# Attention over a small state and a squared-ReLU feed-forward layer on one core: sums of w_out blocks on VectorE, some squares on ScalarE, a new written order from the third batch on

## The chip, the cores and the metric

The kernel runs on one core of a Trainium2 chip. The metric is the device time of one execution in microseconds (us). TensorE (PE) multiplies, VectorE (DVE), ScalarE (ACT) and GpSimd (POOL) do the elementwise work, SyncE (SP) issues nearly all DMAs. A difference of about 0.3% is what a measurement of this kernel can tell from none.

## The reference, cut to what matters

```python
# attention: B, H, S, Ns, D = 8, 8, 512, 32, 64
scores = scale * x @ state.T                 # a = softmax(scores); xread = a @ state
scores2 = scale * state @ x.T                # a2 = softmax(scores2); sread = a2 @ x
x = concat([xread, sread], axis=2)           # 8 x 8 x 544 x 64 -> 4352 x 512
# feed-forward: d_model 512, d_ff 2048
h = maximum(x @ w_in, 0.0)
out = (h * h) @ w_out
```

All data are float32. The weights come to the chip as 64-bit floats and are turned into 32-bit ones there.

## The kernel before, in words

The rows of one batch (512 tokens, xread) are a block, numbered 0 to 7; the 256 sread rows of all batches are block 8. TensorE multiplies in a reduced 32-bit format, so each factor is split: hi is the rounded value (a copy on ScalarE), lo is the remainder (one subtraction on VectorE or GpSimd), and a product is hi*hi + hi*lo + lo*hi, three matmuls.

For a block, `hidden(blk, fc)` makes 128 of the 2048 hidden columns (fc counts to 16): six matmuls of 128x512 into `ph`, ReLU on ScalarE into `r`, the square, and the split into `g_hi` and `g_lo`. `accumulate(blk, fc)` multiplies them by 128 rows of w_out (`wo`) into four accumulators. This is done for blocks 0 to 4 and 8; block 8 is worked on between 4 and 5.

Blocks 5 to 7 use seven products in place of eight, as in Strassen's scheme. Once blocks 4 and 8 no longer need two neighbouring `wo` blocks, `sums.p` (`add_weights(p)`, p from 0 to 7) turns them into sums and differences `v`, `sv`, `one`, and splits these in place into `wo`, `both` and `first` (or `two_first`). That is nine operations on VectorE or GpSimd for each p and four casts on ScalarE. `hidden_fast` leaves the squares in a tile `g`; `fast.blk.p.h` (`accumulate_fast`, h is 0 or 1) makes the matching sums of `g` in a tile `s` (f_sum 256, d_sum 256 and e_sum 128 columns) and the remainders `a_g_lo` (p_lo and f_lo, 256 columns each) and `b_g_lo` (b_lo, 384 columns), and issues 21 matmuls of 128x256 into `m`. A step 5.3 in the text is block 5, p = 3, and 5.3.0 its half h = 0.

What runs in which order: `PLAN` is a list of step names; each time a name stands in it, that step's function runs to its next `yield`. So PLAN sets the order in which instructions are written, and a scheduler keeps most of it. Each engine works through its own instructions in order. `SECOND` is a table of keys: an operation whose key stands in it goes to the second engine of its `pick(key, first, second)`. Before the change `add_weights` picks GpSimd first and no key of it stands in the table, and the sums in `accumulate_fast` pick VectorE first, again without a key. The profile names line 408, a wrapper, for every instruction, so tiles tell what an instruction is.

Of the kernel before, what the change touches and what calls it, by code (L numbers as in the profile page):

```python
# [122 lines left out]
        accumulate.1.15 accumulate.1.15 load.3.1 hidden.2.0 hidden.2.0 hidden.2.3 hidden.2.0 hidden.2.0
        accumulate.1.15 accumulate.1.15 load.3.1 load.3.1 accumulate.1.15 accumulate.1.15 hidden.2.3 hidden.2.3
        hidden.2.3 split_wf.4 accumulate.1.15 accumulate.2.0 hidden.2.3 hidden.2.3 prep.3.0 split_wf.4 later_w2.4
        later_w2.4 load.3.1 later_w2.4 later_w2.4 accumulate.2.1 exp_s.2.1 transposes.2 hidden.2.2 transposes.2
        load_wf.1.6 later_w2.4 later_w2.4 later_w2.4 hidden.2.2 hidden.2.2 hidden.2.2 load_w2.2.3 load.4.1
# [5 lines left out]
        hidden.2.5 transposes.2 split_wf.7 split_wf.6 later_w2.6 split_wf.7 later_w2.6 split_wf.7 later_w2.6
        later_w2.6 later_w2.6 later_w2.6 later_w2.6 split_wf.7 load_wf.2.1 later_w2.6 later_w2.6 accumulate.2.5
        load_w2.2.4 load_w2.2.4 later_w2.7 later_w2.7 later_w2.7 later_w2.7 later_w2.7 later_w2.7 later_w2.7
        accumulate.2.6 hidden.2.9 hidden.2.9 load.4.1 load.4.1 hidden.2.9 hidden.2.9 hidden.2.9 hidden.2.9
        hidden.2.7 sread.1 hidden.2.7 hidden.2.7 load_w2.2.5 hidden.2.7 read.2 load_w2.2.6 hidden.2.7 hidden.2.7
        sread.2 load.4.1 sread.2 sread.2 hidden.2.8 hidden.2.8 hidden.2.8 hidden.2.8 later_w2.7 hidden.2.8
        hidden.2.8 accumulate.2.7 w2.1+scores.3 last_w2.1 transposed_scores.3.0 exp_s.3.0 accumulate.2.8 later_w2.7
        last_w2.1 sread.2 start.5 start.5 load_wf.2.0 start.5 start.5 load_w2.2.5 last_w2.1 last_w2.1 load_w2.2.6  # L140
        last_w2.1 load_w2.2.5 hidden.2.11 hidden.2.11 hidden.2.11 load.5.1 softmax.3.0 hidden.2.11
        transposed_scores.3.1 softmax.3.1 load_w2.2.6 exp_s.3.1 prep.4.1 hidden.2.10 hidden.2.10 hidden.2.11
        hidden.2.11 softmax.3.0 softmax.3.0 softmax.3.0 load.5.1 hidden.2.10 load_w2.2.7 load_w2.3.1 hidden.2.10
        load.5.1 load.5.1 softmax.3.1 load_n.3.0 softmax.3.1 hidden.2.10 hidden.2.10 accumulate.2.9 exp_s.3.1
        softmax.3.1 exp_s.3.0 exp_s.3.0 exp_s.3.1 prep.4.0 hidden.2.13 hidden.2.12 hidden.2.12 hidden.2.13
        hidden.2.13 hidden.2.13 transposes.3 transposes.3 hidden.2.13 hidden.2.13 load_w2.2.7 load_w2.3.0
        load_w2.3.1 accumulate.2.10 load_w2.2.7 accumulate.2.11 hidden.2.14 last_w2.1 hidden.2.12 hidden.2.12
# [5 lines left out]
        prep.5.0 transposes.3 start.6 start.6 load_wf.2.5 softmax.3.1 hidden.3.0 start.6 hidden.2.15 hidden.2.15
        hidden.2.15 softmax.4.0 softmax.4.0 softmax.4.0 accumulate.2.14 exp_s.4.0 hidden.3.2 hidden.3.0 hidden.3.0
        hidden.3.0 hidden.3.0 hidden.3.0 accumulate.2.15 accumulate.2.15 accumulate.2.15 accumulate.2.15
        accumulate.2.15 start.6 exp_s.4.1 load_w2.3.2 exp_s.4.1 exp_s.4.0 exp_s.4.0 transposes.4 transposes.4
        softmax.4.0 load_w2.3.2 softmax.4.0 hidden.3.1 accumulate.2.15 hidden.3.1 hidden.3.1 read.3 sread.3 sread.3
        sread.3 accumulate.2.15 accumulate.2.15 hidden.3.1 hidden.3.1 hidden.3.1 prep.5.1 softmax.4.0 softmax.4.0
        hidden.3.2 hidden.3.2 hidden.3.2 hidden.3.2 hidden.3.2 load.6.1 load_n.4.0 softmax.4.1 transposes.4
        load_w2.3.4 softmax.4.1 load_w2.3.3 transposes.4 load.6.1 accumulate.3.0 accumulate.3.1 softmax.4.1  # L160
        softmax.4.1 hidden.3.3 hidden.3.3 hidden.3.3 load.6.1 hidden.3.3 hidden.3.3 hidden.3.3 hidden.3.4
        load_w2.3.5 hidden.3.4 hidden.3.4 load.6.1 accumulate.3.2 load_w2.3.3 hidden.3.4 hidden.3.4 hidden.3.4
        transposes.4 softmax.4.1 softmax.4.1 w2.2+scores.5 last_w2.2 last_w2.2 transposed_scores.5.0 accumulate.3.3
        load_n.4.1 load_w2.3.4 softmax.4.1 hidden.3.5 last_w2.2 last_w2.2 last_w2.2 last_w2.2 exp_s.5.0 softmax.5.0
        transposed_scores.5.1 exp_s.5.0 exp_s.5.1 softmax.5.0 load_w2.3.5 softmax.5.1 load_w2.3.5 hidden.3.7
        prep.6.0 hidden.3.5 hidden.3.5 exp_s.5.1 exp_s.5.1 hidden.3.5 hidden.3.5 hidden.3.5 hidden.3.7
        accumulate.3.4 load_w2.3.4 softmax.5.0 start.7 hidden.3.7 hidden.3.7 hidden.3.7 hidden.3.7 w2.5+read.4
# [5 lines left out]
        accumulate.3.7 softmax.5.1 last_w2.3 last_w2.3 last_w2.3 transposes.5 hidden.3.9 hidden.3.9
        transposed_scores.6.0 transposed_scores.6.1 exp_s.6.1 exp_s.6.1 softmax.5.1 softmax.5.1 softmax.6.1
        load_w2.3.7 hidden.3.9 hidden.3.9 hidden.3.11 load_w2.3.7 hidden.3.11 hidden.3.9 hidden.3.9 hidden.3.11
        load_w2.4.0 load_w2.4.1 accumulate.3.8 exp_s.6.0 softmax.6.0 softmax.6.0 hidden.3.11 hidden.3.11
        hidden.3.11 exp_s.6.0 hidden.3.10 hidden.3.10 load_w2.3.7 hidden.3.10 exp_s.6.0 transposes.5 load.7.1
# [1389 lines left out]
```

## Time and profile before

| | |
|---|---|
| three runs | 681.49, 683.40, 683.48 us; median 683.4 |
| profiled execution | 680.74 us, span from first to last instruction 679.0 us |
| TensorE busy | 647.4 us (95%) |
| VectorE busy | 502.0 us (74%) |
| ScalarE busy | 379.8 us (56%) |
| GpSimd busy | 217.2 us (32%) |
| DMA | 113.07 MB, mean 167 GB/s |

Busy time is the union of an engine's instructions. A share over the whole span is a mean of stages with different limits; the rows below are taken by stage. Consecutive instructions of VectorE overlap a little, so the distance between two starts is shorter than the duration of one.

### The profile page before, as it was taken

How to read it: one execution, taken by the hardware profiler on the slowest of the kernel's cores; microseconds unless marked ns; L12 is line 12 of the kernel's file. 1: busy time of each engine (PE TensorE's matmuls, PEld its weight loads, DVE VectorE, ACT ScalarE, POOL GpSimd, SP SyncE). 2: the span in 40 equal slices, each digit the busy share in tenths (PEclk: the TensorE clock that was granted, in tenths of full speed). 3: DMA queues.
4: the chain of work that ended last, by engine and by line, in shares of the span. 5: the costliest groups of instructions: out<-in, count | busy, mean ns of one | idle time of the engine just before them, and what ended most of it. 6: DMA issues, size and time to landing. Idle time of an engine off the chain costs nothing. (4 is left out here: it accounts for less than half of the span.)

```text
span 679.0 us, 12256 instructions
## 1 busy us (share of the span) xinstructions
PE 647.4 (95%) x4453; PEld 534.0 (79%) x4453; DVE 502.0 (74%) x951; ACT 379.8 (56%) x790; POOL 217.2 (32%) x173
## 2 busy tenths in 40 slices
...
GB/s 300 305 252 270 274 223 303 275 259 259 173 290 244 196 281 221 218 263 128 318 232 125 48 70 149 65 40 52 41 22 46 94 67 121 100 57 154 63 1 63
DMA packets 153132, 113.07 MB, mean 167 GB/s; under 512 B 93168, under 2 KB 126448, under 8 KB 153072
## 3 DMA queue, kind: packets, MB, share of 16 engines
...
q10 hardware_dynamic: 288, 0.26, 0.1%
q14 instruction: 25, 0.20, 0.1%
...
## 5 line engine op out<-in xcount | busy, mean ns | idle before, releaser
L408 PE MATMUL acc<-wo,g_hi 128*128 128x512 f32 x704 | 204.0, 393 | 0.0
L408 PE MATMUL ph<-k_hi,w 128*128 128x512 f32 x512 | 179.9, 401 | 2.2 <-DVE w L408 1.6
L408 PEld LDWEIGHTS acc<-wo,g_hi 128*128 128x128 f32 x704 | 130.6, 188 | 32.8 <-ACT w2h L408 2.5
L408 PE MATMUL acc<-wo,g_lo 128*128 128x512 f32 x352 | 122.2, 392 | 0.1
L408 PEld LDWEIGHTS ph<-k_hi,w 128*128 128x128 f32 x512 | 97.9, 192 | 25.9 <-DVE w L408 2.3
L408 PE MATMUL ph<-k_lo,w 128*128 128x512 f32 x256 | 102.0, 398 | 0.0
L408 ACT ACTIVATE r<-ph 128x512 f32<-128x512 f32 (+1 forms) x91 | 52.8, 580 | 78.7 <-PE ph L408 69.8
L408 DVE TENSOR_TENSOR g_lo<-ph,g_hi 128x512 fp32r<-128x512 f32 (+1 forms) x95 | 60.4, 639 | 37.7 <-ACT g_hi L408 33.6
L408 ACT ACTIVATE ph<-ph 128x512 f32<-128x512 f32 (+1 forms) x106 | 58.3, 550 | 37.4 <-PE ph L408 28.2
L408 PEld LDWEIGHTS acc<-wo,g_lo 128*128 128x128 f32 x352 | 65.7, 188 | 15.5 <-DVE g_lo L408 0.9
L408 POOL TENSOR_TENSOR w<-w_f,w 128x512 fp32r<-128x512 f32 x23 | 30.4, 1326 | 118.9 <-ACT w L408 118.9
L408 PEld LDWEIGHTS ph<-k_lo,w 128*128 128x128 f32 x256 | 49.2, 192 | 8.3
L408 DVE SCALAR_TENSOR_TENSOR ph<-ph,r 128x512 f32<-128x512 f32 (+1 forms) x43 | 27.9, 649 | 34.1 <-ACT r L408 33.8
L408 DVE TENSOR_TENSOR g<-r 128x512 f32<-128x512 f32 x48 | 41.0, 865 | 11.4 <-ACT r L408 11.2
L408 POOL TENSOR_TENSOR o<-s,s 128x256 f32<-128x256 f32 x2 | 1.4, 728 | 131.6 <-ACT s L408 131.6
L408 POOL TENSOR_TENSOR sp<-sp,m 128x512 f32<-128x512 f32 x20 | 21.5, 1074 | 37.4 <-DVE m L408 34.1
L408 POOL TENSOR_TENSOR wf<-wf,wf_hi 128x512 fp32r<-128x512 f32 x11 | 14.6, 1332 | 56.4 <-ACT wf_hi L408 46.1
L408 ACT CAST g_hi<-ph 128x512 fp32r<-128x512 f32 (+1 forms) x53 | 29.2, 551 | 4.1 <-PE acc L408 2.8
L408 ACT ACTIVATE g_hi<-r 128x512 fp32r<-128x512 f32 (+1 forms) x43 | 25.7, 597 | 6.7 <-PE acc L408 4.3
L408 POOL TENSOR_TENSOR s<-sf,s 128x512 fp32r<-128x512 f32 x11 | 14.1, 1292 | 43.2 <-ACT s L408 42.7
L408 ACT CAST w<-w_f 128x512 fp32r<-128x512 f32 x40 | 24.2, 615 | 3.1 <-DMA w_f<-w_d 2.1
L408 POOL TENSOR_SCALAR dec<-wo_raw 128x512 f32<-128x512 f32 x10 | 21.0, 2103 | 13.0 <-DMA wo_raw<-in_moe_w_out_dram 12.8
...
## 6 DMA issues: line engine op xcount, KB each, us to landing
...
```

The lines of the kernel that those rows point to most:

```text
L408: op = call(*args, **kw)
```

## The change

In `add_weights` the two engines of each `pick` change places: VectorE is the first, GpSimd the second. New keys `v`, `sv` and `sv_lo` send 13 of the 72 operations to GpSimd. New keys `f_sum`, `d_sum`, `e_sum`, `p_lo`, `f_lo` and `b_lo` send 93 of the 288 operations of `accumulate_fast` to GpSimd. New keys `g_sq` send 24 of the 48 squares of blocks 5 to 7 to ScalarE. Some other splits change engines, and PLAN is another list from line 119 of the file on (late in block 1). The rest of the code does the same as before.

```diff
 SECOND = """
+    b_lo: 5.6.1 6.0.0 6.0.1 6.2.1 6.3.0 6.5.0 6.6.0 6.7.0 7.2.1 7.4.0
+    d_sum: 5.3.0 5.4.0 6.0.0 6.1.0 6.1.1 6.2.1 6.4.0 6.5.1 6.6.0 7.0.1 7.1.1 7.3.0 7.4.0 7.4.1 7.5.0 7.5.1 7.6.0
...
+    g_sq: 5.0 5.1 5.2 5.3 5.4 5.5 5.6 5.7 5.8 5.9 5.10 5.11 5.12 5.13 5.14 5.15 6.0 6.1 6.2 6.3 6.6 6.7 6.8 6.11
...
+    sv: 0.2 1.1 1.2
+    sv_lo: 0.0 0.1 0.2 0.3 1.3 2.1 2.3 5.1 7.0
+    v: 0.0
...
-            pick(f"v.{p}.{i}", nc.gpsimd, nc.vector).tensor_add(v[:, i], w[:, 0].bitcast(F32), w[:, 1].bitcast(F32))
-            yield
-        pick(f"sv.{p}.0", nc.gpsimd, nc.vector).tensor_sub(s[:, 0], v[:, 0], v[:, 1])
...
+            pick(f"v.{p}.{i}", nc.vector, nc.gpsimd).tensor_add(v[:, i], w[:, 0].bitcast(F32), w[:, 1].bitcast(F32))
+            yield
+        pick(f"sv.{p}.0", nc.vector, nc.gpsimd).tensor_sub(s[:, 0], v[:, 0], v[:, 1])
...
-            pick(f"sv_lo.{p}.{i}", nc.gpsimd, nc.vector).tensor_sub(w[:, 1], a, w[:, 0].bitcast(F32))
+            pick(f"sv_lo.{p}.{i}", nc.vector, nc.gpsimd).tensor_sub(w[:, 1], a, w[:, 0].bitcast(F32))
...
-        if f"g_sq.{blk}.{fc}" in second:
+        if chosen(f"g_sq.{blk}.{fc}"):
```

The order of instructions, at two places. First VectorE at step 5.3 (block 5). In a row, what an instruction writes stands before the arrow and what it reads behind it; `w_5_5` is the split of a weight tile. Before:

```order
L408 TENSOR_TENSOR g_5_3_5598<-r_7_5650 128x2x256
L408 TENSOR_TENSOR s5.3.0_5689<-g_5_3_5598 128x256
L408 TENSOR_TENSOR a_g_lo5.3.0_5691<-g_5_3_5598,a_g_hi5.3.0_5690 128x256
L408 TENSOR_TENSOR s5.3.0_5689<-g_5_3_5598 128x256
L408 TENSOR_TENSOR s5.3.0_5689<-g_5_3_5598 128x128
L408 TENSOR_TENSOR a_g_lo5.3.0_5691<-s5.3.0_5689,a_g_hi5.3.0_5690 128x256
L408 TENSOR_TENSOR s5.3.1_5701<-g_5_3_5598 128x256
L408 TENSOR_TENSOR b_g_lo5.3.0_5707<-s5.3.0_5689,b_g_hi5.3.0_5706 128x384
```

And VectorE at the same step after the change:

```order
L419 TENSOR_TENSOR s5.3.0_5648<-g_5_3_5571 128x256
L419 TENSOR_TENSOR a_g_lo5.3.0_5650<-g_5_3_5571,a_g_hi5.3.0_5649 128x256
L419 TENSOR_TENSOR a_g_lo5.2.1_5599<-s5.2.1_5597,a_g_hi5.2.1_5598 128x256
L419 TENSOR_TENSOR v_5672<-wo_1513 128x512
L419 TENSOR_TENSOR w_5_5_5676<-w_f_5_5677,w_5_5_5676 128x2x256
L419 TENSOR_TENSOR wo_1359<-sv_5458,wo_1359 128x256
L419 TENSOR_TENSOR b_g_lo5.2.1_5683<-s5.2.1_5597,b_g_hi5.2.1_5682 128x384
L419 TENSOR_TENSOR s5.3.0_5648<-g_5_3_5571 128x128
L419 TENSOR_TENSOR a_g_lo5.3.0_5650<-s5.3.0_5648,a_g_hi5.3.0_5649 128x256
L419 TENSOR_TENSOR b_g_lo5.3.0_5717<-s5.3.0_5648,b_g_hi5.3.0_5716 128x384
```

The square g is gone from VectorE, sums of later p (`v` of p = 6, `wo` of p = 5) stand between the step's operations, and one 256-column sum of 5.3.0 went to GpSimd.

Second GpSimd. Before the change it works on sums during block 5 (here those of p = 5 and 6), and has nothing in blocks 6 and 7:

```order
L408 TENSOR_TENSOR v_5676<-wo_1143 128x512
L408 TENSOR_TENSOR v_5676<-wo_1359 128x512
L408 TENSOR_TENSOR sv_5677<-v_5676 128x512 x2
L408 TENSOR_TENSOR one_5678<-v_5676 128x256
L408 TENSOR_TENSOR wo_1359<-sv_5677,wo_1359 128x256
L408 TENSOR_TENSOR v_5783<-wo_1513 128x512
```

After the change two sums are left to it from step 5.1 on, and a part of the fast blocks' own operations; here in block 6:

```order
L419 TENSOR_TENSOR s6.2.0_6466<-g_6_2_6426 128x256
L419 TENSOR_TENSOR a_g_lo6.2.0_6468<-g_6_2_6426,a_g_hi6.2.0_6467 128x256
L419 TENSOR_TENSOR s6.2.0_6466<-g_6_2_6426 128x128
L419 TENSOR_TENSOR s6.3.0_6528<-g_6_3_6442 128x256
L419 TENSOR_TENSOR a_g_lo6.3.0_6530<-g_6_3_6442,a_g_hi6.3.0_6529 128x256
L419 TENSOR_TENSOR a_g_lo6.3.1_6534<-g_6_3_6442,a_g_hi6.3.1_6533 128x256
L419 TENSOR_TENSOR b_g_lo6.3.0_6564<-s6.3.0_6528,b_g_hi6.3.0_6563 128x384
```

The sums have moved to VectorE, and small operations of every fast step have come to GpSimd.

## Rows read from the trace of the kernel before

**Rows 1.** Windows: each engine's busy us (instructions) by stage, clock, DMA.

```profile
core 0: us, PE busy (x) PEld busy (x) DVE busy (x) ACT busy (x) POOL busy (x), PEclk, DMA share, GB/s
242.00:398.00 156.00, 155.15 (x1211) 122.00 (x1210) 103.95 (x197) 84.09 (x163) 27.14 (x23) 1.00 0.71 198
398.00:455.00 57.00, 56.18 (x271) 45.68 (x270) 30.20 (x55) 34.32 (x89) 35.88 (x30) 1.00 0.27 84
455.00:554.00 99.00, 79.09 (x443) 67.34 (x442) 95.08 (x131) 43.40 (x102) 67.13 (x56) 0.88 0.14 46
554.00:616.00 62.00, 61.62 (x427) 57.30 (x427) 50.05 (x126) 31.52 (x69) 0.00 (x0) 1.00 0.32 103
```

**Rows 2.** Timeline of TensorE, the first matmuls of blocks 5, 6 and 7: start, us.

```profile
455.39 0.40 PE L408 MATMUL m<-wo,a_g_hi5.0.0_5324 128*128 128x256 f32 x2
...
553.83 0.40 PE L408 MATMUL m<-wo,a_g_hi6.0.0_6208 128*128 128x256 f32 x2
...
615.91 0.40 PE L408 MATMUL m<-wo,a_g_hi7.0.0_7000 128*128 128x256 f32 x2
```

**Rows 3.** Waits of TensorE, 455 to 554 us: us, times, longest.

```profile
PE m L408 <- DVE a_g_lo5.3.0_5691 L408: 4.4, 2, 2.6
```

**Rows 4.** Waits of TensorE, 554 to 616 us.

```profile
PE m L408 <- DVE a_g_lo6.0.0_6209 L408: 0.4, 1, 0.4
```

**Rows 5.** Timeline of VectorE from 492 us, step 5.3.0: start, us.

```profile
492.17 1.40 DVE L408 TENSOR_TENSOR s5.3.0_5689<-g 128x256 f32<-128x256 f32 x1
493.49 1.48 DVE L408 TENSOR_TENSOR a_g_lo5.3.0_5691<-g,a_g_hi5.3.0_5690 128x256 fp32r<-128x256 f32 x1
494.89 2.76 DVE L408 TENSOR_TENSOR s5.3.0_5689<-g 128x256 f32<-128x256 f32 x2
497.58 0.94 DVE L408 TENSOR_TENSOR a_g_lo5.3.0_5691<-s5.3.0_5689,a_g_hi5.3.0_5690 128x256 fp32r<-128x256 f32 x1
```

**Rows 6.** Timeline of GpSimd in the same stretch.

```profile
491.55 3.14 POOL L408 TENSOR_TENSOR v<-wo 128x512 f32<-128x512 f32 x2
494.77 2.74 POOL L408 TENSOR_TENSOR sv<-v 128x512 f32<-128x512 f32 x2
497.47 0.77 POOL L408 TENSOR_TENSOR one<-v 128x256 f32<-128x256 f32 x1
```

**Rows 7.** Timeline of VectorE in block 7, GpSimd idle.

```profile
637.55 0.56 DVE L408 TENSOR_TENSOR b_g_lo7.3.0_7338<-s7.3.0_7316,b_g_hi7.3.0_7337 128x384 fp32r<-128x384 f32 x1 [0.32 <-ACT b_g_hi7.3.0_7337 L408]
638.02 0.42 DVE L408 TENSOR_TENSOR s7.3.1_7320<-g 128x256 f32<-128x256 f32 x1
638.76 0.69 DVE L408 TENSOR_TENSOR g<-r 128x512 f32<-128x512 f32 x1 [0.32 <-ACT r L408]
639.37 0.42 DVE L408 TENSOR_TENSOR a_g_lo7.3.1_7322<-g,a_g_hi7.3.1_7321 128x256 fp32r<-128x256 f32 x1
...
652.93 0.42 DVE L408 TENSOR_TENSOR s7.5.0_7472<-g 128x256 f32<-128x256 f32 x1
653.27 0.28 DVE L408 TENSOR_TENSOR s7.5.1_7500<-g 128x128 f32<-128x128 f32 x1
653.47 0.42 DVE L408 TENSOR_TENSOR a_g_lo7.5.1_7502<-s7.5.1_7500,a_g_hi7.5.1_7501 128x256 fp32r<-128x256 f32 x1
```

**Rows 8.** GpSimd's groups, 455 to 554 us: busy, mean ns | idle before.

```profile
L408 POOL TENSOR_TENSOR sv<-v 128x512 f32<-128x512 f32 x10 | 14.9, 1504 | 0.4
...
L408 POOL TENSOR_TENSOR wo<-sv,wo 128x256 fp32r<-128x256 f32 x12 | 11.3, 953 | 6.2 <-ACT wo L408 6.1
```

**Rows 9.** The page's groups, whole span: mean ns of GpSimd and ScalarE.

```profile
L408 ACT ACTIVATE r<-ph 128x512 f32<-128x512 f32 (+1 forms) x91 | 52.8, 580 | 78.7 <-PE ph L408 69.8
...
L408 POOL TENSOR_TENSOR o<-s,s 128x256 f32<-128x256 f32 x2 | 1.4, 728 | 131.6 <-ACT s L408 131.6
...
L408 POOL TENSOR_TENSOR s<-sf,s 128x512 fp32r<-128x512 f32 x11 | 14.1, 1292 | 43.2 <-ACT s L408 42.7
```

**Rows 10.** Timelines of VectorE and TensorE at step 7.7.1.

```profile
669.09 0.42 DVE L408 TENSOR_TENSOR a_g_lo7.7.1_7683<-s7.7.1_7681,a_g_hi7.7.1_7682 128x256 fp32r<-128x256 f32 x1
...
671.18 0.28 PE L408 MATMUL m<-wo,a_g_lo7.7.1_7683 128*128 128x256 f32 x1
```

More of the change, by code (lines that the diff above doesn't have):

```diff
@@ L123 @@
[L123 to L127, printed above, removed]
@@ L133 @@
[L133 to L137, printed above, removed]
@@ L138 @@
[L138 to L147, printed above, removed]
@@ L153 @@
[L153 to L162, printed above, removed]
@@ L163 @@
[L163 to L167, printed above, removed]
@@ L173 @@
[L173 to L177, printed above, removed]
@@ new lines @@
+        hidden.2.0 hidden.2.0 accumulate.1.15 accumulate.1.15 accumulate.1.15 accumulate.1.15 accumulate.1.15
+        exp_s.2.1 hidden.2.0 hidden.2.0 hidden.2.0 hidden.2.0 accumulate.1.15 accumulate.1.15 accumulate.1.15
+        accumulate.1.15 accumulate.1.15 load.3.1 load.3.1 hidden.2.1 hidden.2.1 accumulate.2.0 hidden.2.1
+        split_wf.4 exp_s.2.1 hidden.2.1 hidden.2.1 hidden.2.1 exp_s.2.0 exp_s.2.0 transposes.2 split_wf.5
+        later_w2.4 split_wf.5 later_w2.4 transposes.2 later_w2.4 later_w2.4 later_w2.4 later_w2.4 load_wf.1.6
@@ new lines @@
+        later_w2.7 later_w2.7 hidden.2.6 hidden.2.6 hidden.2.6 load.4.1 hidden.2.6 hidden.2.6 hidden.2.6 hidden.2.8
+        hidden.2.8 hidden.2.8 hidden.2.8 hidden.2.8 hidden.2.8 load_w2.2.5 read.2 sread.2 load_w2.2.5
+        accumulate.2.6 later_w2.7 later_w2.7 later_w2.7 sread.2 load_w2.2.6 sread.2 w2.1+scores.3 last_w2.1 start.5
+        start.5 prep.4.0 last_w2.1 last_w2.1 last_w2.1 last_w2.1 transposed_scores.3.0 softmax.3.0 exp_s.3.0
+        load_w2.2.7 load_w2.2.6 load_wf.2.0 accumulate.2.7 start.5 start.5 hidden.2.9 hidden.2.9 hidden.2.9
@@ new lines @@
+        accumulate.2.14 accumulate.2.15 transposes.4 transposes.4 start.6 start.6 load.6.1 accumulate.2.15
+        accumulate.2.15 accumulate.2.15 accumulate.2.15 accumulate.2.15 accumulate.2.15 accumulate.2.15 hidden.3.1
+        load.6.1 hidden.3.0 hidden.3.0 softmax.4.0 load.6.1 load.6.1 read.3 sread.3 sread.3 hidden.3.1 sread.3
+        transposes.4 sread.3 hidden.3.1 hidden.3.2 hidden.3.1 hidden.3.1 hidden.3.1 hidden.3.2 hidden.3.2
+        hidden.3.2 hidden.3.2 hidden.3.2 load_wf.2.5 accumulate.3.0 accumulate.3.1 hidden.3.3 hidden.3.3 hidden.3.3
@@ new lines @@
+        sums.2 sums.2 sums.2 sums.2 hidden.8.14 hidden.8.14 hidden.8.14 hidden.8.15 hidden.8.15 hidden.8.15
+        hidden.8.15 hidden.8.15 sums.2 sums.2 sums.2 sums.2 sums.2 accumulate.8.12 accumulate.8.13 hidden.8.14
+        hidden.8.14 hidden.8.14 hidden.8.14 hidden.8.14 hidden.5.1 hidden.5.1 hidden.5.1 load_w2.5.2 sums.3 sums.3
+        sums.3 sums.3 sums.3 sums.3 hidden.5.0 sums.3 hidden.5.0 load_w2.5.2 load_w2.5.3 sums.3 hidden.5.0
+        fast.5.0.0 load_w2.5.2 accumulate.8.14 accumulate.8.15 accumulate.8.15 sums.4 accumulate.4.15 sums.3 sums.4
@@ new lines @@
+        fast.5.0.0 fast.5.0.0 sums.3 hidden.5.3 sums.3 sums.3 fast.5.0.1 fast.5.0.0 fast.5.0.0 hidden.5.3
+        hidden.5.3 hidden.5.5 fast.5.0.0 sums.3 hidden.5.5 fast.5.0.0 fast.5.0.0 fast.5.0.0 sums.4 fast.5.0.1
+        fast.5.0.1 fast.5.0.1 fast.5.0.1 hidden.5.2 hidden.5.2 fast.5.0.1 hidden.5.2 sums.4 sums.4 sums.4 sums.4
+        sums.4 fast.5.0.0 fast.5.0.0 fast.5.0.0 fast.5.0.0 fast.5.0.0 fast.5.0.1 fast.5.0.1 fast.5.1.0 fast.5.1.0
+        fast.5.0.1 sums.5 fast.5.0.1 fast.5.1.0 load_w2.5.3 hidden.5.4 accumulate.8.15 accumulate.8.15 fast.5.0.1
@@ new lines @@
+        fast.5.0.1 hidden.5.4 fast.5.1.1 fast.5.0.1 fast.5.0.1 hidden.5.4 load_w2.5.3 hidden.5.7 fast.5.1.0
+        fast.5.1.0 fast.5.1.0 fast.5.1.1 fast.5.1.0 fast.5.1.0 fast.5.1.0 fast.5.1.1 fast.5.1.1 fast.5.1.1
+        fast.5.1.1 fast.5.1.1 load_w2.5.4 load_w2.5.4 load_w2.5.4 sums.4 sums.4 fast.5.1.0 sums.5 sums.4 fast.5.1.0
+        fast.5.1.0 sums.4 fast.5.1.0 fast.5.1.0 fast.5.1.1 fast.5.1.1 fast.5.1.1 sums.5 hidden.5.7 hidden.5.7
+        hidden.5.5 sums.5 fast.5.2.0 hidden.5.6 hidden.5.6 fast.5.1.1 fast.5.1.1 fast.5.2.1 fast.5.2.1 fast.5.2.1
@@ new lines @@
+        fast.5.2.1 fast.5.1.1 fast.5.1.1 fast.5.2.1 fast.5.2.1 hidden.5.6 fast.5.2.0 fast.5.2.0 hidden.5.9
+        fast.5.2.0 fast.5.2.0 fast.5.2.0 fast.5.2.0 sums.5 sums.5 fast.5.2.0 fast.5.2.0 fast.5.2.0 hidden.5.9
+        sums.4 fast.5.2.0 fast.5.3.0 fast.5.3.0 fast.5.3.0 fast.5.2.1 fast.5.2.0 fast.5.2.0 fast.5.2.0 fast.5.3.0
+        hidden.5.8 sums.6 load_w2.5.5 load_w2.5.5 load_w2.5.5 sums.5 fast.5.2.1 fast.5.2.1 fast.5.2.1 fast.5.3.0
+        fast.5.3.0 fast.5.3.0 sums.5 sums.5 hidden.5.8 hidden.5.8 fast.5.2.1 fast.5.2.1 fast.5.2.1 fast.5.2.1
@@ new lines @@
+        fast.5.3.0 fast.5.3.0 fast.5.3.0 fast.5.3.0 fast.5.3.0 sums.6 fast.5.3.1 fast.5.3.1 fast.5.3.1 fast.5.3.1
+        fast.5.3.1 fast.5.3.1 fast.5.3.1 sums.5 sums.5 hidden.5.10 sums.5 fast.5.3.1 fast.5.3.1 fast.5.3.1
+        hidden.5.9 hidden.5.10 hidden.5.10 fast.5.3.1 fast.5.3.1 fast.5.3.1 fast.5.3.1 fast.5.3.0 fast.5.3.0
+        fast.5.4.0 fast.5.4.0 sums.6 sums.6 sums.6 fast.5.4.1 fast.5.4.1 fast.5.4.0 fast.5.4.0 fast.5.4.0 sums.5
+        fast.5.4.0 hidden.5.11 load_w2.5.6 load_w2.5.6 load_w2.5.6 fast.5.4.0 fast.5.4.0 fast.5.4.0 hidden.5.11
@@ new lines @@
+        accumulate.8.15 sums.7 fast.5.4.1 fast.5.4.1 fast.5.4.1 sums.6 sums.6 sums.6 sums.6 fast.5.4.1 fast.5.4.1
+        sums.6 sums.6 fast.5.4.0 fast.5.4.0 hidden.5.13 hidden.5.13 fast.5.4.0 fast.5.4.1 fast.5.4.1 fast.5.4.1
+        fast.5.4.1 sums.7 sums.7 fast.5.4.0 fast.5.4.0 hidden.5.11 fast.5.5.0 fast.5.5.0 fast.5.5.0 fast.5.4.1
+        fast.5.5.1 fast.5.4.1 fast.5.4.1 fast.5.5.0 hidden.5.13 sums.6 fast.5.5.0 fast.5.5.0 fast.5.5.0 fast.5.5.0
+        fast.5.5.1 fast.5.5.1 fast.5.5.1 fast.5.5.1 hidden.5.12 hidden.5.12 hidden.5.12 fast.5.5.0 sums.7 sums.7
@@ new lines @@
+        load_w2.5.7 fast.5.5.0 sums.7 fast.5.5.0 load_w2.5.7 fast.5.5.0 fast.5.5.0 fast.5.5.1 fast.5.5.1 sums.6
+        fast.5.5.1 fast.5.5.1 fast.5.5.0 fast.5.6.0 fast.5.6.0 fast.5.6.0 fast.5.6.0 fast.5.5.1 fast.5.5.1
+        load_w2.6.0 load_w2.6.1 load_w2.5.7 fast.5.6.1 fast.5.6.1 fast.5.6.0 fast.5.6.0 fast.5.6.0 fast.5.6.1
+        fast.5.6.1 fast.5.6.1 fast.5.5.1 fast.5.5.1 fast.5.5.1 sums.7 sums.7 sums.7 hidden.5.15 hidden.5.15
+        fast.5.6.0 fast.5.6.0 sums.7 fast.5.6.0 fast.5.6.0 hidden.5.14 load_k.6 fast.5.6.1 fast.5.6.1 fast.5.6.1
@@ new lines @@
+        fast.5.6.1 sums.7 sums.7 fast.5.6.1 fast.5.6.1 hidden.5.14 fast.5.6.0 hidden.5.15 hidden.5.14 sums.7
+        fast.5.7.0 fast.5.7.0 fast.5.7.0 fast.5.7.0 fast.5.6.1 fast.5.6.1 fast.5.6.1 fast.5.6.0 fast.5.6.0
+        fast.5.7.0 fast.5.7.0 fast.5.7.0 load_k.6 fast.5.7.1 load_k.6 load_k.6 load_k.6 fast.5.7.1 fast.5.7.0
+        fast.5.7.0 fast.5.7.0 fast.5.7.0 hidden.6.0 fast.5.7.1 fast.5.7.0 fast.5.7.1 load_w2.6.2 fast.5.7.1
+        fast.5.7.0 fast.5.7.0 fast.5.7.0 fast.5.7.0 fast.5.7.1 fast.5.7.1 fast.5.7.1 fast.5.7.0 fast.5.7.0
@@ new lines @@
+        fast.6.3.0 fast.6.2.0 fast.6.2.0 fast.6.3.1 fast.6.2.0 fast.6.3.1 fast.6.3.0 fast.6.3.0 hidden.6.8
+        fast.6.3.0 fast.6.3.1 hidden.6.9 fast.6.3.0 fast.6.3.0 fast.6.3.0 fast.6.3.0 fast.6.3.0 fast.6.3.0
+        fast.6.3.1 fast.6.3.1 fast.6.3.0 fast.6.3.0 load_w2.6.6 load_w2.6.7 hidden.6.9 hidden.6.9 fast.6.4.1
+        fast.6.3.1 fast.6.3.1 fast.6.3.1 fast.6.3.1 fast.6.4.1 hidden.6.11 fast.6.4.1 fast.6.3.1 fast.6.3.1
+        hidden.6.11 hidden.6.11 hidden.6.10 fast.6.3.1 fast.6.4.0 fast.6.4.0 fast.6.4.0 fast.6.4.0 fast.6.4.0
@@ new lines @@
+        fast.6.4.0 fast.6.3.1 hidden.6.10 fast.6.4.0 fast.6.4.0 fast.6.4.1 fast.6.4.0 fast.6.4.0 hidden.6.13
+        fast.6.4.0 fast.6.4.1 fast.6.4.1 fast.6.4.0 fast.6.4.0 fast.6.4.1 hidden.6.13 hidden.6.13 fast.6.4.1
+        fast.6.4.1 fast.6.4.0 fast.6.4.1 fast.6.4.1 hidden.6.10 fast.6.5.0 fast.6.5.0 fast.6.4.1 fast.6.5.0
+        fast.6.5.1 fast.6.5.1 fast.6.5.0 fast.6.5.0 fast.6.5.0 fast.6.5.0 fast.6.5.1 fast.6.5.1 fast.6.5.1
+        fast.6.4.1 fast.6.4.1 hidden.6.12 hidden.6.12 fast.6.5.1 fast.6.5.0 fast.6.5.1 fast.6.5.0 fast.6.5.0
@@ new lines @@
+        fast.6.6.0 hidden.7.0 hidden.7.0 fast.6.7.0 fast.6.6.0 fast.6.6.0 fast.6.7.0 fast.6.7.0 fast.6.7.0
+        fast.6.7.0 fast.6.7.0 fast.6.7.1 fast.6.7.1 fast.6.7.1 fast.6.7.0 fast.6.7.0 fast.6.7.0 hidden.7.1
+        hidden.7.1 fast.6.7.0 fast.6.7.0 fast.6.7.0 fast.6.7.0 fast.6.7.0 fast.6.7.1 fast.6.7.1 fast.6.7.1
+        fast.6.7.0 fast.6.7.0 fast.6.7.0 fast.6.7.1 fast.6.7.1 hidden.7.1 fast.7.0.0 fast.6.7.1 fast.7.0.0
+        fast.7.0.0 fast.7.0.0 load_w2.7.1 hidden.7.3 fast.6.7.1 fast.6.7.1 fast.7.0.0 fast.7.0.0 fast.7.0.0
@@ new lines @@
+        fast.6.7.0 fast.6.7.0 hidden.7.3 fast.6.7.0 fast.6.7.0 fast.6.7.0 hidden.7.2 fast.6.7.1 fast.6.7.1
+        load_w2.7.2 fast.7.0.0 fast.6.7.1 fast.6.7.1 load_w2.7.3 fast.6.7.1 hidden.7.2 hidden.7.2 fast.7.0.1
+        fast.7.0.1 fast.6.7.0 fast.6.7.0 fast.7.0.1 fast.7.0.1 fast.6.7.1 fast.6.7.1 fast.6.7.1 hidden.7.4
+        hidden.7.4 load_w2.7.4 fast.7.0.0 fast.7.0.0 fast.7.0.0 fast.7.0.1 hidden.7.3 fast.7.0.1 fast.7.0.1
+        fast.7.0.0 fast.7.0.0 fast.7.0.1 fast.7.0.1 fast.7.0.1 fast.7.0.1 fast.7.0.0 fast.6.7.1 hidden.7.5
```

370 lines of the change are left out of this document (172 added, 198 removed), and 6 rows, old and new, of the table SECOND.

## The prediction

> **What bounds the kernel now.** I read the stages first, then the stretch in which TensorE falls behind. In the stages [rows 1] TensorE is busy nearly all the time, but for one: from 455 to 554 us it is busy 79.1 of 99 us, at a mean granted clock of 0.88. That is block 5, the first of the three blocks that use the sums of w_out. Its eight steps begin at 455.39 and those of block 6 at 553.83, so they take 98.4 us; the same work in block 6 takes 62.1 us, until block 7 begins at 615.91 [rows 2]. Block 6 is TensorE at its peak: it waits 0.4 us there in all [rows 4]. So up to 36.3 us of the span lie in block 5, and no other stage has as much to give: from 242 to 398 TensorE is busy 155.15 of 156 us and from 398 to 455 us 56.18 of 57 [rows 1].
>
> What TensorE waits for in block 5 are mostly split remainders a_lo of VectorE, 4.4 us for those of step 5.3.0 alone [rows 3], and VectorE is busy 95.1 of the 99 us there [rows 1]. It isn't short of work slots, it is slowed: a 128x256 subtraction starts at 492.17, the next at 493.49, the next at 494.89, so a step of 1.36 us [rows 5], while GpSimd runs its 128x512 additions at the same time [rows 6]. With GpSimd idle the next instruction starts 0.34 us after a 128x256 one, 0.61 after 128x512, 0.47 after 128x384, 0.20 after 128x128 [rows 7]. So one 128x512 operation of GpSimd takes 1.36 - 0.34 = 1.02 us away from VectorE. A 128x256 one takes 0.94 - 0.42 = 0.52: that is what the subtraction at 497.58 lasts beyond its undisturbed 0.42 [rows 5 to 7]. All these instructions read two tensors in SBUF.
>
> Does this price account for the block? VectorE's own rows between the remainders of step 5.0 and of 6.0 are 74 of 256 columns, 16 of 128, 16 of 384 and 20 of 512: 25.2 + 3.2 + 7.5 + 12.2 = 48.1 us. GpSimd has 31 operations of 512 columns and 25 of 256 in that stage (two of the nine groups are shown [rows 8]): 31 x 1.02 + 25 x 0.52 = 44.6. Together 92.7 of 98.4 us; 5.7, or 5.8%, are left for waits on ScalarE. So VectorE, with what GpSimd takes from it, is the bound of block 5.
>
> The Trainium skill ("SBUF — State Buffer", Who interferes with whom) says that a VectorE instruction with two SBUF inputs and a GpSimd instruction that reads SBUF shut each other out for the whole instruction. The rows agree in kind; in size they show 1.02 and 0.52, not GpSimd's whole 1.29 and 0.73 [rows 9]. By the rule block 5 would need 48.1 + 31 x 1.29 + 25 x 0.73 = 106.3 us, more than the 98.4 that it took. I go by the rows.
>
> **The change part by part.**
> Sums: of 72 operations 59 go to VectorE and 13 stay on GpSimd. Squares g of blocks 5 and 6: 24 of 32 leave VectorE for ScalarE, all 16 of block 5. In return 93 of the small sums and remainders of the fast blocks go to GpSimd: 14 in block 5, 46 in block 6, 33 in block 7.
>
> Block 5, counted in the new order between the same marks. VectorE: 74 of 256 columns, 12 of 128, 13 of 384, 25 of 512, so 25.2 + 2.4 + 6.1 + 15.3 = 49.0 us. Nearly what it was: the squares that left and the sums that came balance, partly since the first sums are now made earlier. GpSimd: 14 of 256 columns at 0.52, 4 of 128 and 3 of 384. The last two sizes stand in no row; of 128 it is over nothing and under 0.52, I take the middle, 0.26; of 384 between 0.52 and 1.02, I take 0.77. That makes 7.3 + 1.0 + 2.3 = 10.6. The sum is 59.6 where it was 92.7; with the same 5.8% of waits 63.3 us. TensorE needs 62.1. Two engines in a chain with nearly equal loads and two or three buffers between them will not both be full, so I take more: 66 us, midway between 63.3 and the 68 us that GpSimd's whole durations would give (0.73, and 0.45 and 1.0 for the sizes between [rows 9]: 49.0 + 15.0 = 64.0, with 5.8% 68). Block 5 gains 98.4 - 66 = 32.4 us.
>
> Ahead of the last remainder of step 5.0 stand 31 of VectorE's 59 sums, 21 of 512 columns and 10 of 256: 12.8 + 3.4 = 16.2 us. It is busy 30.2 of 57 us in the stage before block 5 [rows 1], so some 46 of 57 now; cost 0, up to 16 if that cover were gone. What is queued behind a late sum on VectorE are block 8's remainders g_lo, for which TensorE waits next.
>
> Block 6: VectorE's rows fall to 28.3 us (47 of 256, 5 of 128, 11 of 384, 10 of 512) and GpSimd takes 28 x 0.52 + 11 x 0.26 + 5 x 0.77 = 21.4 (44 operations lie between these marks); 49.7 of 62.1 us. Before it was 49.1 (77, 16, 16 and 20 rows of these sizes) without GpSimd, and TensorE waited 0.4 us [rows 4]. So the load stays; only each moved operation is answered later. I take 1 us lost over blocks 6 and 7 (block 7: 23.7 + 15.6 = 39.3 of some 52).
>
> ScalarE: 16 squares of about 0.58 us [rows 9] are 9.3 us on top of 43.4 in block 5 [rows 1]: 52.7 of 66, not the bound. The tail: the last remainder of step 7.7.1 moves to GpSimd; before it starts at 669.09 and its matmul at 671.18 [rows 10], so 1.7 us of cover for some 0.3 to 0.9 more; cost 0.
>
> Blocks 2 to 4 are written in another order with some splits on other engines. TensorE waits there for almost nothing, so there is nothing to win; VectorE is busy 103.95 of 156 us and GpSimd 27.14 [rows 1], so I take 0, with 3 us of loss as the bound.
>
> Sum: 680.7 us of the profiled execution (span 679.0 and 1.7 around it) - 32.4 + 1 = 649.3. The three runs have a median 2.7 us higher; on that scale 652.
>
> **The rivals.**
> *TensorE's floor.* If the first sums lie far enough ahead, block 5 runs like block 6: 680.7 - 36.3 = 644.4, on the median's scale 647. For it: sums are independent of block 5 and can fill VectorE's gaps. Against: 63.3 is above 62.1 even without jitter. 20%.
>
> *GpSimd shuts VectorE out for its whole instruction, as the skill's page has it.* Block 5 takes 68; in block 6 28.3 + 28 x 0.73 + 11 x 0.45 + 5 x 1.0 = 58.7 us, with 5.8% 62.3, so TensorE's 62.1 has no room left and it loses about 4 us as I took for block 5, and 2 in block 7. 680.7 - 30.4 + 6 = 656.3, on the median's scale 659. With half of the 16 us at the seam to block 8, 667. For it: durations of 1.4 to 1.6 us on VectorE are seen beside GpSimd. Against: the account of block 5 above. 22%.
>
> *Slower: the small operations on GpSimd become what TensorE waits for.* A remainder takes 0.42 us on VectorE and 0.73 on GpSimd, and waits up to 0.6 for an instruction of VectorE: up to 0.9 us later, 79 times in blocks 6 and 7. If TensorE waited each time, 71 us: 680.7 - 32.4 + 71 = 719, 722 on the median's scale. It decides once about 36 of the 79 are waited for in full. For it: only three buffers each of hi and lo. Against: about 1.4 us of hidden matmuls stand between steps, and VectorE's own load in blocks 6 and 7 falls. 4%.
>
> *No change.* The wait moves to the seam, and block 5's chain stays serial through ScalarE: the 32 us of gain are used up by 16 there and as much in blocks 5 to 7: 683. 3%.
>
> **How the numbers follow.** The forecast has 51%, with 648 to 657 its own range. Below it the floor is 647, and since 3 us may go either way in blocks 2 to 4 I begin at 644; above, the shut-out with half the seam reaches 667, and I end at 668. Less than 2 in 10 lie outside. Faster by over 0.3% (2 us, what a measurement of this kernel can tell) 0.93, same 0.03, slower 0.04.
>
> **What would show it.** After the change, the first matmuls of steps 5.0 and 6.0 should lie about 66 us apart, with a granted clock of 1.00 in that stretch; the clock falls now in the stretches where TensorE idles (0.88 on average from 455 to 554). VectorE's 128x256 operations should mostly last 0.42 us in block 5, and 0.9 beside GpSimd in block 6. Block 6 should stay at 62 to 64 us. I am wrong if TensorE's waits in blocks 6 and 7 name GpSimd remainders for more than 5 us, if the stage before block 5 grows by more than 3 us, or if blocks 2 to 4 do.

## The result and the profile after

| | before | after |
|---|---|---|
| median | 682.44 us (4 runs, 680.95 to 683.48) | 655.93 us (4 runs, 655.29 to 657.07) |
| profiled execution, span | 679.0 us | 653.5 us |
| ratio | | 0.9615, 95% interval 0.9589 to 0.9641 |

The change makes the kernel 26 us faster; forecast were 652 us, with 644 to 668 as the range. The stages of the changed kernel, from the windows view (columns as in [rows 1]), cut at the first matmul of block 8, of block 5, of block 6 and of block 7:

```profile
403.59:462.87 59.28, 58.25 (x280) 47.28 (x278) 42.08 (x83) 40.76 (x102) 14.76 (x14) 1.00 0.30 89
462.87:527.04 64.17, 63.39 (x434) 58.40 (x433) 60.34 (x134) 47.24 (x108) 18.82 (x17) 1.00 0.21 68
527.04:590.79 63.75, 63.21 (x434) 58.48 (x432) 40.52 (x74) 37.12 (x82) 35.53 (x46) 1.00 0.30 93
```

Block 5 takes 64.2 us where it took 98.4 [rows 2], TensorE is busy in 63.4 of them at a granted clock of 1.00; before it was 0.88 in that stretch [rows 1]. The first matmuls, from TensorE's timeline, that these cuts stand for:

```profile
462.87 0.40 PE L419 MATMUL m<-wo,a_g_hi5.0.0_5337 128*128 128x256 f32 x2
...
527.04 0.28 PE L419 MATMUL m<-wo,a_g_hi6.0.0_6249 128*128 128x256 f32 x1
...
590.79 0.28 PE L419 MATMUL m<-wo,a_g_hi7.0.0_6979 128*128 128x256 f32 x1
```

What answers to [rows 5] is VectorE at step 5.3 now (timeline; start, duration). The sums `v` and `both` stand between the step's operations, and all rows shown have their undisturbed durations: 0.42 us for 256 columns, 0.68 for 512. GpSimd is idle in this stretch; where it works again, from 489.10 us on, two `sv` of VectorE take 2.10 us in place of 1.29. In the whole of block 5, 70 of VectorE's 79 operations of 256 columns last 0.45 us at most; before, 43 of 73 did.

```profile
485.79 0.68 DVE L419 TENSOR_TENSOR v<-wo 128x512 f32<-128x512 f32 x1
486.39 0.42 DVE L419 TENSOR_TENSOR s5.3.1_5736<-g 128x256 f32<-128x256 f32 x1
486.73 0.42 DVE L419 TENSOR_TENSOR a_g_lo5.3.1_5738<-g,a_g_hi5.3.1_5737 128x256 fp32r<-128x256 f32 x1
487.06 0.62 DVE L419 TENSOR_TENSOR s5.3.1_5736<-g 128x256 f32<-128x256 f32 x2
487.60 0.42 DVE L419 TENSOR_TENSOR a_g_lo5.3.1_5738<-s5.3.1_5736,a_g_hi5.3.1_5737 128x256 fp32r<-128x256 f32 x1
487.94 0.69 DVE L419 TENSOR_TENSOR both<-sv,both 128x512 fp32r<-128x512 f32 x1
```

And what answers to [rows 3] are TensorE's waits in block 5, all that are left of them (us, times, longest):

```profile
PE m L419 <- DVE b_g_lo5.7.1_6172 L419: 0.3, 1, 0.3
PE m L419 <- DVE b_g_lo5.2.1_5683 L419: 0.3, 1, 0.3
PE m L419 <- POOL a_g_lo5.4.1_5802 L419: 0.2, 1, 0.2
```

By stage, from the profiled executions: block 5 gives 34.3 us; block 8 starts 5.9 us later (403.59 against 397.67); the stage from there to block 5 is 1.6 longer (59.28 against 57.72), of which 1.4 are one hidden step, six matmuls of 0.23, that now stands ahead of step 5.0; block 6 is 1.7 longer (63.75 against 62.1); the rest is 0.3 shorter. 34.3 - 5.9 - 1.6 - 1.7 + 0.3 = 25.4; the spans differ by 25.5. Hidden steps have changed sides of the marks behind as well: block 5 holds 16 of them (17 before), block 6 16 (15) and what follows 11 (12). So 1.4 of the 34.3 us of block 5, and most of the 1.7 of block 6, are such a step and not a gain or a loss.

A correction to the description of the change: lines of the table of engines run on into a second line, and some counts there and in the forecast miss these. 35 of the 48 squares of the fast blocks go to ScalarE (16, 10 and 9 of blocks 5, 6 and 7), not 24, and 96 small operations go to GpSimd (14, 46 and 36), not 93. In blocks 2 to 4, 16 squares go to ScalarE and 8 leave it. The rows counted in each engine's order were complete.

### The profile page after: what moved, and what is told of

Its sections match the earlier page's. It is cut to its first block, busy times and chain, and to the rows that moved or that the text cites. A ratio compares the mean times of both kernels' runs of the same rounds, so it can differ in the third digit from the quotient of the medians.

```text
span 653.5 us, 12292 instructions
## 1 busy us (share of the span) xinstructions
PE 636.3 (97%) x4453; PEld 527.2 (81%) x4453; DVE 458.3 (70%) x883; ACT 403.6 (62%) x835; POOL 206.7 (32%) x196
## 4 chain that ended last, share of the span: by engine, by line
PE 78%; DVE 10%; ACT 4%; issue 3%; DMA 2%; POOL 1%; SPq 0%; POOLq 0%; DVEq 0%; ACTq 0%
PE acc L419 32%; PE ph L419 24%; PE m L419 13%; PE w2ps L419 3%; PE w4ps L419 2%; PE pr L419 1%; ACT ph L419 1%; PE st L419 1%; DVE g_lo L419 1%; DVE m L419 1%; DVE v L419 1%; DMA w2a_d<-w2h 1%; PE pw L419 1%; DMA a<-a_d 1%; DMA xn<-in_x_dram 1%
## 5 line engine op out<-in xcount | busy, mean ns | idle before, releaser
L419 PE MATMUL ph<-k_hi,w 128*128 128x512 f32 x512 | 176.6, 394 | 3.9 <-ACT w4o L419 1.3
L419 ACT ACTIVATE ph<-ph 128x512 f32<-128x512 f32 (+1 forms) x124 | 68.3, 551 | 49.3 <-PE ph L419 43.7
L419 ACT ACTIVATE r<-ph 128x512 f32<-128x512 f32 (+1 forms) x82 | 47.5, 580 | 43.7 <-PE ph L419 41.8
L419 POOL TENSOR_TENSOR w<-w_f,w 128x512 fp32r<-128x512 f32 x17 | 23.3, 1368 | 59.7 <-ACT w L419 46.4
L419 ACT CAST g_hi<-ph 128x512 fp32r<-128x512 f32 (+1 forms) x62 | 34.3, 553 | 2.3 <-PE acc L419 0.9
L419 DVE SCALAR_TENSOR_TENSOR ph<-ph,r 128x512 f32<-128x512 f32 (+1 forms) x34 | 21.8, 643 | 14.8 <-ACT r L419 14.6
L419 DVE TENSOR_TENSOR w<-w_f,w 128x512 fp32r<-128x512 f32 x23 | 17.1, 749 | 16.2 <-ACT w L419 16.1
L419 ACT ACTIVATE g<-r 128x512 f32<-128x512 f32 x35 | 21.8, 629 | 0.6
L419 ACT ACTIVATE g_hi<-r 128x512 fp32r<-128x512 f32 (+1 forms) x34 | 20.0, 593 | 3.0 <-PE acc L419 2.5
L419 ACT COPY w4o<-w4ps 128x512 f32<-128x512 f32 x21 | 11.9, 588 | 14.8 <-PE w4ps L419 14.2
```

The source lines that it names most:

```text
L419: op = call(*args, **kw)
```

## Experiments

"Block 5" is in each the time from the first matmul of step 5.0 to that of step 6.0. The runs belong to four questions.

### Which part frees block 5: sums, squares or order?

**The sums back on GpSimd**, all else as changed (the lines `v`, `sv` and `sv_lo` of the table go too):

```diff
-            pick(f"v.{p}.{i}", nc.vector, nc.gpsimd).tensor_add(...)
+            pick(f"v.{p}.{i}", nc.gpsimd, nc.vector).tensor_add(...)
...                                   # likewise sv and sv_lo
```

> The changed kernel with all 72 sums of w_out blocks back on GpSimd; order, squares and small operations stay as changed. Theory 1 (block 5 is bound by VectorE with what GpSimd takes from it): VectorE's own rows between steps 5.0 and 6.0 fall from 49 to 35 us, but GpSimd's sums take some 43 us from them and its small ones 10, so 88 us, with 5.8% of waits 93 us where the changed kernel has 64.2; the time rises by 25 to 32 us to about 685. Rival (the new written order and the squares on ScalarE bring the gain): block 5 stays under 72 us and the time under 664.

Measured 679.53 us, ratio to before 0.9942 (0.9922 to 0.9961); 23.6 over the changed kernel, a little less than the 25 to 32 forecast. Block 5 takes 81.4 us, not 93, and the stage before it is 7.4 us longer than in the changed kernel. Most of the gain hangs on where the sums are made. The size was off: VectorE is busy 68.0 us and GpSimd 54.9 in the 81.4, so here neither is full. What VectorE's instructions last beyond their undisturbed durations adds up to 28.6 us, where the forecast had some 53 and the changed kernel has 6.5. What else holds the block was not taken apart.

```profile
405.28:471.96 66.68, 60.31 (x279) 48.06 (x278) 29.33 (x56) 40.86 (x102) 41.06 (x39) 0.97 0.26 80
471.96:553.33 81.37, 68.95 (x433) 61.64 (x432) 67.97 (x103) 48.00 (x108) 54.87 (x53) 0.96 0.17 53
```

**The sums alone on VectorE, in the old order** (the reverse of the diff above, made in the kernel before):

> The kernel before, old order and old engines, with one part of the change alone: 59 of the 72 sums on VectorE. Theory 1: VectorE's rows in block 5 are 65.5 us and GpSimd's five others take 5 from them, with 5.8% of waits 75 us where before has 98.4; the time falls by some 23 us to 659 (654 to 665). Rival (the old order was chosen for GpSimd's sums, so that sums on VectorE stand in the way of the steps' own operations): block 5 stays over 90 us and the time over 674.

Measured 670.87, ratio 0.982 (0.9801 to 0.984): between the two theories. Block 5 takes 81.9 us with VectorE busy 77.7 of them, and the stage before it 63.6 (57.7 before).

**Sums and squares, in the old order** (the lines of `g_sq` are added to the table as well):

> As the one before, and the 35 squares of the fast blocks on ScalarE as in the changed kernel; no small operation on GpSimd, old order. Theory 1: VectorE's rows in block 5 are 55.9 us and GpSimd takes 5, with 5.8% 64.8 us, near TensorE's 62.1, so 65 to 67 us; blocks 1 to 4 keep the old order and do not lose the 5 us that they lose in the changed kernel; time about 650 (647 to 655), under the 655.9 of the changed kernel. Rival (the small operations on GpSimd and the new order are needed for the gain): 660 or more.

Measured 666.8, ratio 0.9757 (0.9729 to 0.9785). The rival was right: with the changed kernel's engines for sums and squares, but the old order, 16 us are gained, where the new order without small operations on GpSimd (next question) gains 29. Block 5 takes 74.1 us with VectorE busy 65.6, and the stage before it 66.5 where before has 57.7:

```profile
397.94:464.42 66.48, 60.12 (x274) 48.35 (x273) 38.41 (x77) 38.17 (x96) 21.46 (x18) 0.95 0.24 73
464.42:538.50 74.08, 66.34 (x439) 59.85 (x438) 65.64 (x152) 49.71 (x113) 14.62 (x8) 1.00 0.19 60
```

VectorE is busy 38 of 66 us in the first of these stretches, so it isn't work that is too much there but its place. TensorE's waits in it are for block 8's remainders and a ReLU of ScalarE, 6.2 us in all:

```profile
PE ph L413 <- DVE g_lo L413: 3.2, 3, 1.7
PE ph L413 <- ACT r L413: 3.0, 1, 3.0
```

The longest shows how they come about (timelines of ScalarE, VectorE and TensorE). ScalarE's copy `cross` is done at 450.0 us; the subtraction of block 8 on VectorE that reads it starts at 453.27, behind sums of later steps, and ScalarE and TensorE wait for it:

```profile
449.64 0.37 ACT L413 COPY cross<-ph 128x256 f32<-128x256 f32 x1
...
450.19 0.69 DVE L413 TENSOR_TENSOR both<-sv,both 128x512 fp32r<-128x512 f32 x1
450.80 1.23 DVE L413 TENSOR_TENSOR v<-wo 128x512 f32<-128x512 f32 x1
452.06 1.29 DVE L413 TENSOR_TENSOR sv<-v 128x512 f32<-128x512 f32 x2
453.27 0.43 DVE L413 TENSOR_TENSOR ph<-ph,cross 128x256 f32<-128x256 f32 x1
...
453.73 0.37 ACT L413 ACTIVATE ph<-ph 128x256 f32<-128x256 f32 x1 [3.41 <-DVE ph L413]
...
454.65 0.79 PE L413 MATMUL ph<-k_hi,w 128*128 128x512 f32 x1 [3.04 <-ACT r L413]
```

After this wait TensorE's granted clock is 0.50, the lower of its two levels (1.2 and 2.4 GHz), from 455 to 460 us. The run with the sums alone has the same waits there, but a clock of 1.00 in the stage, and the stage is 2.9 us shorter: about 3 of the 8.8 us are the clock.

**The order alone**, with every engine as before:

```diff
-    g_sq: 5.0 5.1 5.2 ...        # and all other keys that are new
+                                 # SECOND and the picks of the kernel before
```

> The written order of the changed kernel with all engines as before: sums on GpSimd, squares on VectorE, no small operation on GpSimd. Theory 1 (engines decide, order is second): block 5 is as slow as before or slower, 95 us and more, time 683 or more. Rival (the order alone brings a good part): under 675.

Measured 694.23, ratio 1.0179 (1.0138 to 1.0219): slower than before by 1.8%. Block 5 takes 91.5 us, better than before and under the 95 of theory 1, but the stage ahead of it 69.7 and the front up to block 8 409.25. So neither order nor engines bring the whole gain alone: sums and squares bring 16 us in the old order (666.8 against 683.1, measured beside it), and 41 lie between 694.2 and 652.8, the run with no small operation on GpSimd (next question), in the new one. These 41 aren't sums and squares alone: the two runs differ in other splits too, and in the profiled executions 6.1 us lie ahead of block 8 (409.25 against 403.12).

**The squares back on VectorE** in the changed kernel (the lines of `g_sq` go):

> The changed kernel with the 35 squares of the fast blocks on VectorE again. Theory 1: VectorE's rows in block 5 rise from 49 to 58.6 us, with GpSimd's measured 6.4 and 5.8% of waits 69 us where the changed kernel has 64.2; block 6 has room (34 + 11 of 62); the time rises by 4 to 6 us to about 661. Rival (squares on VectorE are hidden, since TensorE is the bound by now): within 1.5 us of 655.9.

Measured 669.02, ratio 0.9794 (0.9771 to 0.9818): 13 us, twice the forecast; 9.8 of them lie in block 5, the rest in the stages around it. Block 5 takes 73.9 us with VectorE busy 70.7 of them, 96%. VectorE is the bound again:

```profile
465.63:539.56 73.93, 65.95 (x433) 58.84 (x432) 70.69 (x151) 39.33 (x93) 17.81 (x18) 1.00 0.21 65
```

### What are the small operations on GpSimd worth?

**All 96 back on VectorE** in the changed kernel:

```diff
-    b_lo: 5.6.1 6.0.0 6.0.1 ...
-    d_sum: 5.3.0 5.4.0 6.0.0 ...
...                               # likewise e_sum, f_lo, f_sum and p_lo
```

> The changed kernel with the 96 small sums and remainders of the fast blocks back on VectorE; sums, squares and order stay. Theory 1a (GpSimd's price on VectorE is 1.02 us per 512 columns and 0.52 per 256, so moving small operations away hardly relieves VectorE and only delays answers): VectorE's rows in block 5 rise from 48.6 to 54.8 us, GpSimd's 6.4 fall to about 1; the time stays within 2 us of the changed kernel's 655.9, and blocks 6 and 7 lose 1 to 2 us less. Theory 1b (VectorE is full at some 87% of own rows and extension, which the two last kernels showed: 87% and 88%): 55.8 / 0.87 = 64.1 in block 5, no longer over TensorE's 62.1 by less than now, so 656 to 659. Rival (the small operations on GpSimd carry a good part of the gain): 663 or more.

Measured 652.77, ratio 0.956 (0.9545 to 0.9576); the interval of the changed kernel lies above it. The 96 operations cost 3 us. Theory 1a holds but for the size of its bound, theory 1b (656 to 659) doesn't, and TensorE is busy in every one of block 5's 62.5 us:

```profile
462.00:524.54 62.54, 62.54 (x434) 58.19 (x432) 59.07 (x148) 48.05 (x108) 3.96 (x2) 1.00 0.22 69
524.54:587.20 62.66, 62.66 (x434) 58.41 (x432) 44.73 (x118) 36.63 (x81) 0.00 (x0) 1.00 0.30 96
```

Beside the changed kernel's rows this measures the price. In block 5 VectorE is busy 59.1 us where it does the 14 operations itself and 60.3 where GpSimd does them: it is no freer. In block 6 it is busy 44.7 where it does the 46 itself and 40.5 where GpSimd does. These are 28 of 256, 11 of 128 and 7 of 384 columns, on VectorE 28 x 0.34 + 11 x 0.20 + 7 x 0.47 = 15.0 us [rows 7]. So 46 operations and 35.5 us of GpSimd relieve VectorE by 4.2 us, and 10.8 come back as longer instructions (11.1, added up over VectorE's instructions); TensorE loses 1.1 us in the block.

**Squares and small operations back on VectorE**, where VectorE is the bound of block 5 (both diffs):

> The changed kernel with the 35 squares and the 96 small operations back on VectorE: beside the run with the squares back alone (669.0) it shows what small operations on GpSimd are worth where VectorE is the bound of block 5. Theory (GpSimd takes from VectorE about what it takes over): the 14 operations of block 5 add some 6 us of own rows and take away some 7 us of extension, blocks 6 and 7 are 1 to 2 us shorter; 665 to 669. Rival (they relieve a full VectorE): 672 or more.

Measured 668.59, ratio 0.9781 (0.9735 to 0.9826), not to be told from 669.02 with the small operations on GpSimd. Block 5 takes 73.7 and 73.9 us. Where VectorE is full, small operations on GpSimd don't relieve it either.

### Where do the 5.9 us ahead of block 8 come from?

**The old front**: order and engines of the kernel before up to block 8, then those of the changed one.

```diff
 PLAN = """
-        softmax.2.1 softmax.2.1 softmax.2.0 ...   # the changed list up to hidden.8.0
+        softmax.2.1 softmax.2.1 start.3 ...       # the old list up to there, then the rest
...
-    w4_out: 0.1 1.3 2.2 3.1 3.3 5.1 5.3 6.0 6.3 7.0 7.1
+    w4_out: 0.1 1.3 2.2 3.1 3.3 4.0 4.2 6.0 7.1 7.3
...                     # likewise square, w2_lo and k_lo of batches 2 to 4, out, sm_mul, sm_sub, wf_lo
```

> Up to the first hidden step of block 8 the written order and the engines of the kernel before, from there on those of the changed kernel. Theory (blocks 1 to 4 lose about 5 us in the changed kernel by remainders g_lo and evacuations on ScalarE that come late, apart from block 5): the first matmul of block 8 comes at 398 instead of 403.6 us and the rest is as in the changed kernel, 650 to 652 us. Rival (what the front leaves behind on VectorE and ScalarE is needed by the seam to block 5): the front gains 5 us and the seam loses them again, 655 or more.

Measured 650.89, ratio 0.954 (0.9524 to 0.9556): 5 us, as forecast. The first matmul of block 8, from the timelines of the kernel before, the changed one and this one:

```profile
397.67 0.50 PE L408 MATMUL ph<-sr_k_hi,s 128*128 128x512 f32 x2
```
```profile
403.59 0.73 PE L419 MATMUL ph<-sr_k_hi,s 128*128 128x512 f32 x3
```
```profile
398.46 0.73 PE L454 MATMUL ph<-sr_k_hi,s 128*128 128x512 f32 x3
```

In the changed kernel TensorE waits from 20 to 403 us for these, 4.2 us in all, where this run waits 0.2:

```profile
PE ph L419 <- ACT w4o L419: 1.3, 2, 0.7
PE acc L419 <- DVE g_lo L419: 1.1, 1, 1.1
PE ph L419 <- DVE w2l L419: 1.1, 1, 1.1
PE ph L419 <- DVE g_lo L419: 0.7, 2, 0.4
```

The order costs them: with the order alone, and all engines as before, block 8 starts at 409.25, later still (in an execution 4 us over its kernel's median), so the new engines of the front win a part back. The new engines in the old order weren't tried.

### Do the gains add up?

**Old front and no small operation on GpSimd** (both diffs):

> Old front as in the run before last, and the small operations of the fast blocks on VectorE. If both theories hold (the front's 5 us and the small operations' near nothing add up): 650 to 654. If the small operations are needed: 658 or more.

Measured 648.82, ratio 0.951 (0.9494 to 0.9525): faster than the changed kernel and than before, and 1.2 us under the 650 forecast as the lower end. Of 8 us that would add up, 7.1 are there.

**And the last 13 sums on VectorE too** (the lines `v`, `sv` and `sv_lo` go):

> The kernel with the old front and no small operations on GpSimd, and the 13 sums that were left on GpSimd on VectorE too. GpSimd's 13 stand ahead of block 5 for the most part and lengthen VectorE's instructions there by 2.3 us; their own rows on VectorE would be some 5 us. Theory (VectorE has room ahead of block 5, TensorE is the bound from block 8 on): 647 to 650, no difference from 648.8 beyond 0.3%. Rival (the seam is full): 651 or more.

Measured 648.07, ratio 0.9491 (0.9452 to 0.9529), not to be told from the run before. Without any operation of GpSimd in blocks 5 and 6, block 5 takes 62.5 us, all of them TensorE's:

```profile
457.86:520.38 62.52, 62.52 (x434) 58.23 (x432) 59.10 (x150) 47.96 (x108) 0.00 (x0) 1.00 0.22 69
```

## Why the prediction was right, and where it was off

On the profiled executions 649.3 us were forecast and 655.3 measured: 5.9 more ahead of block 8, 1.6 in the stage before block 5, 0.3 behind it, and 1.9 less in block 5. The total, 655.9 by the medians, lies between the forecast's 652 and the 659 of the shut-out rival and doesn't decide between them; block 5 does.

**Block 5 is bound by VectorE with what GpSimd takes from it: right.** Added up over VectorE's instructions of block 5, the time beyond their undisturbed durations (0.28, 0.42, 0.56 and 0.69 us by size) is 42.8 us before, where the forecast's price gave 44.6, and 6.5 after. With their own steps from start to start [rows 7], 49.2 and 53.0 us in sum, that makes 92.0 of 98.4 us and 59.4 of 64.2. Taking either of the two moves back, sums or squares, brings the block to 73.9 or more. VectorE's busy share doesn't show this by itself: it is 84 to 96% wherever block 5 is longer than 64.2 us, but 94% also in the changed kernel and with no small operation on GpSimd, where TensorE is the bound. TensorE's granted clock rose with the change, from 0.88 to 1.00 in block 5; VectorE was idle for 3.9 of the 98.4 us before, so the lower clock can have added little on top of its work. It wasn't measured apart.

**The term of block 5, 66 us: 64.2.** The gain was 34.3 where the forecast had 32.4. The account, 59.6 us of VectorE with what GpSimd takes, came out at 59.4, in part by luck: between the first matmuls VectorE's own rows are 53.0 us, not 49.0, and GpSimd took 6.5, not 10.6. Too careful was the allowance for two nearly equal queues.

**The seam ahead of block 5, taken as 0: right in the sum, by a reason that fails.** The forecast took it as 0 because VectorE had room there, and gave the written order no term. In the changed kernel the stage is 1.6 us longer, 1.4 of it the hidden step. But with sums and squares on the same engines in the old order the seam cost 8.8 us (66.5 against 57.7) with VectorE busy 38 us of it, and block 5 takes 9.9 more than in the changed kernel, 1.4 of it a hidden step. Room on an engine that works in order counts only where no one waits for what is queued behind: the step that fails is the one that read cover from busy time.

**Blocks 2 to 4, taken as 0 with 3 us as the bound: wrong, 5.9.** This is the term that was missized; that they would grow by more than 3 us was named as a sign of being wrong, and it came true. The forecast argued that TensorE waits for nothing there, so nothing can be won; it can lose, and VectorE's and ScalarE's free time again said nothing about it. The old front gives 5 us back.

**GpSimd's price: somewhat high in block 5, about double in block 6.** 1.02 and 0.52 us came from a stretch in which both engines always had work. Between the first matmuls of block 5 lie 17 operations of GpSimd, 8.3 us by that price, and VectorE's instructions grew by 6.5. In block 6 they grew by 11.1 instead of 21.4, and those of 256 columns beside GpSimd last 0.68 us on average, not 0.9: VectorE is busy only 40.5 of 63.8 us there, so GpSimd often meets it idle.

**Small operations: 1 us lost over blocks 6 and 7 was forecast, 1.3 shown** (from the first matmul of block 6 to the end, with as many hidden steps as before); putting all 96 back gives 3.2 with those of block 5. The rival in which TensorE waits for GpSimd's remainders appears only in traces: 0.2 us in block 5 and 0.5 in block 6.

**The rule of the Trainium skill ("SBUF — State Buffer", Who interferes with whom), whole instructions:** its rival had block 5 at 68 and block 6 short of room; measured 64.2 and 63.75. That section of the Trainium skill calls the lock exclusive and says that a VectorE instruction with two SBUF inputs contends; its words on the whole instruction stand beside VectorE's 2-port mode. The two do get in each other's way here, but an operation of GpSimd cost VectorE less than its length on average, and as little as 0.15 us (below).
